# Third products, transposes and logits over all 128 rows of the array, in an mLSTM and mixture-of-experts kernel

## The chip, the cores and the metric

The kernel runs on one core of one Trainium2 chip. The metric is the device time of one execution in microseconds (us). A profile holds one execution, instruction by instruction: PE is TensorE's matmul, PEld its weight load (the stationary operand; it overlaps PE), DVE is VectorE, ACT ScalarE, POOL GpSimd, SP SyncE, which issues most DMAs. "L682" is a line of the kernel before.

## The reference

Two parts, in float32. First a recurrent attention (mLSTM) over batch 4, 8 heads, 768 steps, head size 40:

```python
    for t in range(S):
        m_new = np.maximum(f_gate[:, :, t] + m, i_gate[:, :, t])
        ...
        C = f_stab[:, :, None, None] * C + i_stab[:, :, None, None] * np.einsum('bhd,bhe->bhde', vt, kt)
        n = f_stab[:, :, None] * n + i_stab[:, :, None] * kt
        ...
        y[:, :, t] = o * h_tilde / denom
```

The eight heads side by side make 3072 tokens of 320 numbers. Each goes to one of 16 experts, in two choices of four (a group, then an expert in it), and through that expert's two layers:

```python
            h = np.maximum(xg[mask_e] @ w1[g, e], 0.0)
            ye = h @ w2[g, e]
            ...
            out[tok_idx] = combined[:, None] * ye
```

w1 is 320 x 1024 and w2 1024 x 320 for each expert.

## The kernel before, in words

A token's 320 columns are two blocks of 128 and one of 64. This third block is what the change is about.

**Attention.** The 768 steps are cut in 6 chunks of 128, for 4 batches: 24 units `u`, each 128 tokens. A unit makes scores (`sp`, L190), the carried state's part (`it`, L216), the new state (`st`, L236) and the values (`av`, L264) on TensorE; DVE and POOL mask and normalize, and `x` (L299) holds the finished tokens. `turn` (L302 on) lets ACT copy columns 256 to 319 once more to 320 to 383, stores the 384 columns in `x_d`, transposes `x` in three pieces (`tp`, L312; the third has 64 columns), and ACT copies them out to `xT` in two instructions (L318, L319). `logits` (L324 on) multiplies `xT` with `wc`, 20 columns, in three products (L333): xT is the stationary operand, and in the third it has 64 rows. `route` makes from four units' logits the choice, the rank in the expert (`lg`, L375 to L384) and the place in a table `itab`.

**Experts.** They are taken by falling number of tokens. `CAPS[r]` is the number of slots that the r-th gets: 384 (256 early and 128 late), 352, 320, 288, four of 256, four of 192, three of 160, and 128. The tokens of an expert are gathered in blocks of 128 slots (`load_x`, L593), the last block of some with fewer: 96 for expert 1, 64 for experts 2 and 8 to 11, 32 for 3 and 12 to 14. Slots that no token took hold the number of a row of zeros. `turn_tasks` transposes each gathered block (`tpm`, L648). Most experts then split x and w1 into two fp32r parts and use columns 256 to 319, doubled, against `wsk`. The experts in `FULL`, 13 to 15, don't: they multiply fp32 by fp32 in `expert` (L682), with three products per block of 128 hidden columns, of 128, 128 and 64 rows. Each fp32 product shows as two loads and two matmuls. Two blocks of hidden columns share a PSUM tile (`psh`, three buffers); ACT and DVE take the relu and its remainder from it (L668, L671), and a part of the next expert's w2 is split (`between`; L611, L613). Then come the next expert's transposes (`then`), and w2's products (`po`, L735 to L741).

**What sets the order.** Up to unit 21 the order is as written (`manual_schedule`); from there on a scheduler orders by its priorities. Each engine works through its own queue in order.

Of the kernel before, what the change touches and what calls it, by code (L numbers as in the profile page):

```python
# [18 lines left out]
P = 128  # L19
# [3 lines left out]
DM = H * D  # L23
NTOK = B * S
NE = 16
F = 1024
# [30 lines left out]
def lstm_moe(ctx: ExitStack, tc: tile.TileContext, gates, qkT, nat, og, wcat, w1, w2, cst, out):  # L57
    nc = tc.nc
    enter = ctx.enter_context
    mm = nc.tensor.matmul  # L60
# [3 lines left out]
    x_d = dram.tile([NTOK + 1, ROW], F32, name="x_d")  # L64
# [7 lines left out]
    ident = cs[:, C_ID:C_ID + P]  # L72
# [5 lines left out]
    wc = const.tile([P, 3, 20], F32, name="wc")  # L78
# [33 lines left out]
    rt = {"manual": True}  # L112
# [19 lines left out]
    st_ = {}  # L132
# [169 lines left out]
    def turn(u):  # L302
        c, b = divmod(u, B)
        x = st_[u]["x"]
        nc.scalar.copy(x[:, DM:DM + 64], x[:, 256:DM])
        rt["xs"] = ins = nc.sync.dma_start(x_d[b * S + c * P:b * S + (c + 1) * P, :], x)
        if c == NCH - 1:
            no_order("early", ins)
        tp = ps_1.tile([P, 3, P], F32, name="tp", tag="tp")
        for k in range(3):  # L310
            kk = min(P, DM - k * P)
            ins = nc.tensor.transpose(out=tp[0:kk, k, :], in_=x[:, k * P:k * P + kk], identity=ident)  # L312
        rt["tp", u] = ins
        if u > NU - 4:
            with tc.issue_after(ins.ins):
                busy(2)
        xT = wk.tile([P, 3, P], F32, name="xT")
        nc.scalar.copy(xT[:, 0:2, :], tp[:, 0:2, :])  # L318
        nc.scalar.copy(xT[0:64, 2, :], tp[0:64, 2, :])  # L319
        st_[u]["xT"] = xT  # L320


# [2 lines left out]
    def logits(u):  # L325
        c, b = divmod(u, B)
        if b == 0:
            rt["bank"] = ps_1.tile([P, B * 36 + NE], F32, name="lg")
        if u == NU - 1:
            rt["bank"] = ps_1.tile([P, B * 36 + NE], F32, name="lg2", tag="av")  # L330
        for k in range(3):
            kk = min(P, DM - k * P)
            rt["lg", u] = mm(rt["bank"][:, b * 20:(b + 1) * 20], st_[u]["xT"][0:kk, k, :], wc[0:kk, k, :],  # L333
                             start=(k == 0), stop=(k == 2))

        ends = {B - 1: 0} if c < NCH - 2 else {B - 2: 0, B - 1: B - 1}
        if b in ends:
            chores.insert(0 if c < NCH - 2 else len(chores), route(c, ends[b], b + 1, rt["bank"]))
# [90 lines left out]
    def no_order(key, ins):  # L429

        for o in unordered.setdefault(key, []):
            tc.declare_no_dep(ins.ins, o.ins, reason="distinct rows")
        unordered[key].append(ins)
# [116 lines left out]
    def gather(o, src, idx):  # L550
        return nc.gpsimd.indirect_dma_start(out=o, out_offset=None, in_=src,  # L551
                                            in_offset=bass.IndirectOffsetOnAxis(ap=idx, axis=0))
# [36 lines left out]
    def load_x(W, idx, early=False):  # L589
        xg = []  # L590
        for i, m in enumerate(blocks(W)):
            g = mxp.tile([P, ROW], F32, name="xg", bufs=9)
            ins = gather(g[0:m], x_d, idx(i, m)[:, 0:1])  # L593
            if early:

                no_order("early", ins)
            xg.append(g)
        return xg
# [37 lines left out]
    def turn_tasks(key, W, xg, banks=None):  # L636
        t = {}

        def one(i, m):
            if i == 0:  # L640
                pool = pools["xhl"][len(xhls) % len(pools["xhl"])]
                sh, dt = ([P, 3, W], F32) if key[0] in FULL else ([P, 3, 2, W], F32R)
                t["x"] = xhls[key] = pool.tile(sh, dt, name="xhl", bufs=1)
            xhl, g = t["x"], xg[i]
            pool, tag = (banks or ((ps_1, "tp"), (ps_1, "lg"), (ps_1, "av")))[i]
            tp = pool.tile([P, 3, P], F32, name="tpm", tag=tag)
            for k in range(3):
                nc.tensor.transpose(out=tp[:, k, 0:m], in_=g[0:m, k * P:(k + 1) * P], identity=ident[0:m, 0:m])  # L648
            if key[0] in FULL:
                nc.scalar.copy(xhl[:, :, i * P:i * P + m], tp[:, :, 0:m])  # L650
                return
            xh = xhl[:, :, 0, i * P:i * P + m]
            nc.scalar.copy(xh, tp[:, :, 0:m])
            nc.vector.tensor_tensor(xhl[:, :, 1, i * P:i * P + m], tp[:, :, 0:m], xh.bitcast(F32), op=ALU.subtract)

        return [lambda i=i, m=m: one(i, m) for i, m in enumerate(blocks(W))]

    def expert(key, W, ws, xg, idx, between=(), then=None, last=None):
        xhl = xhls[key]
# [15 lines left out]
        if key[0] in FULL:  # L675
            w1s = w1st[key[0]]
            for f in range(0, NF, 2):
                ps = pools["ps_h"].tile([P, 512], F32, name="psh")
                for g in range(2):
                    for k in range(3):  # L680
                        kk, s = min(P, DM - k * P), slice(k * F + (f + g) * P, k * F + (f + g + 1) * P)
                        ins = mm(ps[:, g * W:(g + 1) * W], w1s[0:kk, s], xhl[0:kk, k, :], start=(k == 0), stop=(k == 2))  # L682
                relu(f, 2, ps[:, 0:2 * W].rearrange("p (q w) -> p q w", q=2))
                do(between, 1)
        elif key in NARROW:
            xw, xh = [xhl[:, k].rearrange("p a w -> p (a w)") for k in range(3)], [xhl[:, k, 0, :] for k in range(2)]
            for f in range(0, NF, 2):
                hs = pools["hp"].tile([P, 2, W], F32, name="hs", bufs=2)
                for g in range(2):
                    ps = pools["ps_h"].tile([P, 512], F32, name="psh")  # L690
                    s0 = slice((f + g) * P, (f + g + 1) * P)
                    s1 = slice(F + (f + g) * P, F + (f + g + 1) * P)
                    mm(ps[:, 0:2 * W], w1h[:, s0], xw[0], start=True, stop=False)
                    mm(ps[:, 0:W], w1l[:, s0], xh[0], start=False, stop=False)
                    mm(ps[:, 0:W], w1l[:, s1], xh[1], start=False, stop=False)
                    mm(ps[:, 0:2 * W], w1h[:, s1], xw[1], start=False, stop=False)
                    ins = mm(ps[:, 0:2 * W], wsk[:, s0], xw[2], start=False, stop=True)
                    nc.scalar.copy(hs[:, g, :], ps[:, W:2 * W])
                    nc.vector.tensor_tensor(hs[:, g, :], hs[:, g, :], ps[:, 0:W], op=ALU.add)
                act = relu(f, 2, hs)  # L700
                if key[0] == 0:
                    do(between, 1)
        else:
            per = 2 if W <= 256 else 1
            for f in range(0, NF, per):
                ps = pools["ps_h"].tile([P, 512], F32, name="psh")
                for g in range(per):
                    s0 = slice((f + g) * P, (f + g + 1) * P)
                    s1 = slice(F + (f + g) * P, F + (f + g + 1) * P)
                    xh, xl = [xhl[:, k, 0, :] for k in range(3)], [xhl[:, k, 1, :] for k in range(3)]  # L710
                    todo = [(w1h, s0, xh[0]), (w1h, s0, xl[0]), (w1h, s1, xh[1]), (w1h, s1, xl[1]), (wsk, s0, xh[2]),
                            (wsk, s0, xl[2]), (w1l, s0, xh[0]), (w1l, s1, xh[1])]
                    for n, (w, s, x) in enumerate(todo):
                        ins = mm(ps[:, g * W:(g + 1) * W], w[:, s], x, start=(n == 0), stop=(n == len(todo) - 1))  # L714
                relu(f, per, ps[:, 0:per * W].rearrange("p (q w) -> p q w", q=per))
                if per == 2 or f % 2:
                    do(between, 1)
# [6 lines left out]
        for i, m in enumerate(blocks(W)):  # L724
# [3 lines left out]
            for f in range(NF):  # L728
                s = slice(f * DM, (f + 1) * DM)
# [4 lines left out]
                if m > 64:  # L734
                    mm(po[0:m], hh[:, f, t], w2h[:, s], start=st0, stop=False)  # L735
                    mm(po[0:m], hh[:, f, t], w2l[:, s], start=False, stop=False)  # L736
                    ins = mm(po[0:m], hh[:, f, tl], w2h[:, s], start=False, stop=sp0)  # L737
# [293 lines left out]
    with tc.For_i(0, nv, 1):  # L1031
# [25 lines left out]
        g = mxp.tile([P, ROW], F32, name="xg", bufs=9)  # L1057
        gather(g, x_d, ix[:, 0:1])
        w1s = wst.tile([P, 3 * F], F32, name="w1s")
# [3 lines left out]
        tp = ps_1.tile([P, 3, P], F32, name="tpm", tag="tp")  # L1063
        for k in range(3):
            nc.tensor.transpose(out=tp[:, k, :], in_=g[:, k * P:(k + 1) * P], identity=ident)
        xT = mxp.tile([P, 3, P], F32, name="xhl", bufs=1)
        nc.vector.tensor_copy(xT, tp)
        h = hp.tile([P, NF, P], F32, name="hh")
        for f in range(NF):
            ps = pools["ps_h"].tile([P, 512], F32, name="psh")  # L1070
            for k in range(3):
                kk = min(P, DM - k * P)
                mm(ps[:, 0:P], w1s[0:kk, k * F + f * P:k * F + (f + 1) * P], xT[0:kk, k, :], start=(k == 0),
                   stop=(k == 2))
# [12 lines left out]
def _lay(inputs):  # L1087
# [3 lines left out]
    q, k, v, o = (inputs[n] for n in ('q', 'k', 'v', 'o_gate'))  # L1091
# [12 lines left out]
    og = c(rows(o).reshape(NCH * B, P, DM).transpose(1, 0, 2))  # L1104
    wg, we = inputs['moe_w_group'], inputs['moe_w_expert']
    wcat = np.concatenate([wg, we.transpose(1, 0, 2).reshape(DM, NE)], axis=1)
    wcat = np.concatenate([wcat, np.zeros((3 * P - DM, 20), wcat.dtype)], axis=0)
    wcat = c(wcat.reshape(3, P, 20).transpose(1, 0, 2))
    w1 = inputs['moe_w1'].reshape(NE, DM, F)
    w1 = np.concatenate([w1, w1[:, 2 * P:]], axis=1)  # L1110
# [35 lines left out]
```

## Time and profile before

| | |
|---|---|
| median of 3 executions | 456.69 us (455.43 to 459.14) |
| the profiled execution | 457.81 us, span 456.2 us |
| mean granted TensorE clock | 0.977 |
| busy: PE, PEld | 426.2, 398.7 us |
| busy: DVE, ACT, POOL | 294.6, 253.8, 193.2 us |
| DMA | 94.75 MB, mean 208 GB/s |

How rows read: a group has line, engine, operation, output<-inputs, shapes and count, then busy us and mean ns of one, then the idle time just before and what ended it ("issue": nothing that the profile shows). For PE and PEld, "64*128" is rows times columns of the array that the stationary operand takes; the next "64x160" is the moving operand's partitions by elements. A row of a timeline has start and duration in us, and merges like instructions that follow each other under the first one's shape. A row of the waits has who waited for whom, us in total, how often, and the longest.

### The profile page before, as it was taken

The page shows a single profiled execution, that of the slowest core. Times are in us where ns is not written, and L with a number is a line of the kernel's source. Part 1 is how long each engine was busy: PE and PEld are TensorE (multiplying, and loading weights), DVE is VectorE, ACT ScalarE, POOL GpSimd, SP SyncE. Part 2 cuts the span into 40 slices and gives each one's busy share as a digit, 9 for nine tenths or more (in the row PEclk, how much of TensorE's full clock was granted, in tenths as well). Part 3 has the DMA queues.
Part 4 walks back from the last instruction along what each step waited for, and adds up shares of the span by engine and source line. Part 5 has one row for each costly group of instructions (what it writes and reads, how often), then busy time and mean ns, then how long its engine had stood idle before and what let it go on. Part 6 is the DMA issues. An engine that isn't in the chain of part 4 may idle for free.

```text
span 456.2 us, 9465 instructions
## 1 busy us (share of the span) xinstructions
PE 426.2 (93%) x3420; PEld 398.7 (87%) x3420; DVE 294.6 (65%) x737; ACT 253.8 (56%) x587; POOL 193.2 (42%) x216
## 2 busy tenths in 40 slices
PE   7589999997987999699999999999999999999995
PEld 4489999897987997498999999999999999988784
DVE  6746877658768897495747584676656876772510
ACT  5557666483674842446637464657565765672411
POOL 7544566565564563337713415303330663130110
PEclk9989999998998999599999999999999999999999
DMA  4999797997799922347995536658665776344000
GB/s 153 289 290 284 248 242 227 282 239 247 206 324 298 321 70 60 144 156 215 366 379 185 202 120 236 214 190 293 211 222 187 281 250 218 133 147 141 14 15 10
DMA packets 29909, 94.75 MB, mean 208 GB/s; under 512 B 9169, under 2 KB 13226, under 8 KB 26276
## 3 DMA queue, kind: packets, MB, share of 16 engines
q1 hardware_dynamic: 24660, 78.28, 53.2%
q0 software_dynamic: 4928, 15.49, 10.0%
q8 instruction: 28, 0.46, 0.5%
q10 hardware_dynamic: 272, 0.36, 0.3%
q14 instruction: 21, 0.17, 0.1%
HBM read 84.14 MB, written 10.82 MB: 208 GB/s over the span
## 4 chain that ended last, share of the span: by engine, by line
PE 56%; issue 20%; POOL 11%; DVE 6%; DMA 3%; ACT 2%; POOLq 1%; ACTq 0%; DVEq 0%
PE psh L714 20%; PE po L735 6%; PE po L736 6%; PE po L737 6%; PE sp L190 4%; PE tpm L648 2%; POOL itab L458 2%; POOL sr L293 2%; DMA qk<-in_qkT_dram 2%; PE it L216 2%; PE po L741 2%; POOL ab L152 2%; DMA xg<-x_d,ix 1%; POOL kw L203 1%; PE po L740 1%
## 5 line engine op out<-in xcount | busy, mean ns | idle before, releaser
L551 POOL DMA_INDIRECT xg<-x_d,ix x34 | 41.6, 1223 | 109.0 <-DMA ix<-itab 65.5
L555 POOL DMA_INDIRECT out_dram<-y,ix x34 | 40.8, 1200 | 60.7 <-ACT y L747 42.8
L735 PE MATMUL po<-w2h,hh 128*128 128x320 f32 (+1 forms) x208 | 65.8, 317 | 0.0
L737 PE MATMUL po<-w2h,hh 128*128 128x320 f32 (+1 forms) x208 | 64.2, 309 | 0.0
L736 PE MATMUL po<-w2l,hh 128*128 128x320 f32 (+1 forms) x208 | 64.2, 309 | 0.0
L613 DVE TENSOR_TENSOR w2l<-w2s,w2h 128x640 fp32r<-128x640 f32 x64 | 50.2, 817 | 20.5 <-ACT w2h L611 20.4
L180 ACT ACTIVATE ab<-ab,bcol 128x128 f32<-128x128 f32 x184 | 56.3, 388 | 12.8 <-POOL ab L152 12.3
L714 PE MATMUL psh<-xhl,w1h 128*128 128x256 f32 (+4 forms) x352 | 59.5, 290 | 0.2 <-DVE sm L390 0.2
L671 DVE SCALAR_TENSOR_TENSOR hh<-psh,hh 128x256 fp32r<-128x256 f32 (+2 forms) x104 | 39.5, 411 | 24.3 <-ACT hh L668 23.9
L668 ACT ACTIVATE hh<-psh 128x512 fp32r<-128x512 f32 (+5 forms) x68 | 33.4, 491 | 38.7 <-PE psh L714 21.3
L190 PE MATMUL sp<-qk 128*128 128x128 f32 x384 | 50.8, 287 | 4.4 <-DMA qk<-in_qkT_dram 4.4
L264 PE MATMUL av<-nt,pt 128*128 128x128 f32 x384 | 51.4, 287 | 0.8 <-DVE pt L196 0.7
L190 PEld LDWEIGHTS sp<-qk 128*128 128x128 f32 x384 | 47.2, 199 | 5.2 <-issue 2.6
L714 PEld LDWEIGHTS psh<-xhl,w1h 128*128 128x128 f32 x352 | 50.5, 192 | 1.2 <-ACT ex L357 1.0
L264 PEld LDWEIGHTS av<-nt,pt 128*128 128x128 f32 x384 | 46.3, 196 | 2.2 <-DVE pt L196 1.2
L152 POOL TENSOR_SCALAR_AFFINE_SELECT ab<-ab 128x1024 f32<-128x1024 f32 (+1 forms) x25 | 27.2, 1089 | 48.0 <-DMA ab<-a_d 43.6
L611 ACT CAST w2h<-w2s 128x640 fp32r<-128x640 f32 x64 | 43.2, 723 | 0.0
L735 PEld LDWEIGHTS po<-w2h,hh 128*128 128x128 f32 (+1 forms) x208 | 38.8, 187 | 0.8 <-ACT hh L668 0.2
L196 DVE TENSOR_TENSOR pt<-sp,ab 128x512 f32<-128x512 f32 x48 | 32.8, 684 | 9.8 <-PE sp L190 8.0
L613 DVE TENSOR_TENSOR w1l<-w1s,w1h 128x1024 fp32r<-128x1024 f32 x26 | 31.7, 1219 | 11.1 <-ACT w1h L611 8.8
L736 PEld LDWEIGHTS po<-w2l,hh 128*128 128x128 f32 (+1 forms) x208 | 38.9, 187 | 0.0
L737 PEld LDWEIGHTS po<-w2h,hh 128*128 128x128 f32 (+1 forms) x208 | 38.8, 187 | 0.0
(177 smaller groups left out, 873.4 us busy)
## 6 DMA issues: line engine op xcount, KB each, us to landing
w1s<-in_w_dram SPq DMA_DIRECT2D x12, 1536.0 KB
w2s<-in_w_dram SPq DMA_DIRECT2D x12, 1280.0 KB
ab<-a_d SPq DMA_DIRECT2D x23, 512.0 KB
nt<-in_nat_dram SPq DMA_DIRECT2D x24, 324.0 KB
qk<-in_qkT_dram SPq DMA_DIRECT2D x48, 160.0 KB
x_d<-x SPq DMA_DIRECT2D x24, 192.0 KB
sig<-in_og_dram SPq DMA_DIRECT2D x6, 640.0 KB
w1s<-in_w_dram SPq DMA_DIRECT2D x4, 768.0 KB
```

The lines of the kernel that those rows point to most:

```text
L180: rt["exp"] = nc.scalar.activation(ab[:, j, :], ab[:, j, :], AF.Exp, bias=bcol[:, c, b * H + j:b * H + j + 1])
L190: mm(sp[:, jj, :], qk[:, j % 2, j // 2, :], qk[:, 2, j // 2, :], start=True, stop=True)
L264: mm(av[:, o:o + P], t["pm"][j // 4][:, j % 4, :], nt[:, o:o + P], start=True, stop=True)
L551: return nc.gpsimd.indirect_dma_start(out=o, out_offset=None, in_=src, in_offset=bass.IndirectOffsetOnAxis(ap=idx, axis=0))
L555: return nc.gpsimd.indirect_dma_start(out=out, out_offset=bass.IndirectOffsetOnAxis(ap=idx, axis=0), in_=y, in_offset=None, bounds_check=N ...
L611: nc.scalar.copy(a, src[:, s])
L613: lows.append(lambda: nc.vector.tensor_tensor(o[rows], src[rows, s], a[rows].bitcast(F32), op=ALU.subtract))
L671: nc.vector.scalar_tensor_tensor(hh[:, f:f + per, dst], src[:, :, t], 0.0, hr.bitcast(F32)[:, :, t], op0=ALU.max, op1=ALU.subtract)
L714: ins = mm(ps[:, g * W:(g + 1) * W], w[:, s], x, start=(n == 0), stop=(n == len(todo) - 1))
L735: mm(po[0:m], hh[:, f, t], w2h[:, s], start=st0, stop=False)
L736: mm(po[0:m], hh[:, f, t], w2l[:, s], start=False, stop=False)
L737: ins = mm(po[0:m], hh[:, f, tl], w2h[:, s], start=False, stop=sp0)
```

## The change

`turn` transposes three times 128 columns; the third piece begins at column 192, so that columns 192 to 255 come twice. One copy brings all to `xT`. `wcat` gets its 64 rows of zeros ahead of the last 64 rows instead of behind them, so the doubled columns meet zeros, and all three logit products have 128 rows. Short blocks of slots are gathered with 128 rows, and transposed as 128 x 128; only the first `m` columns of the result are copied out, as before. In FULL experts the third piece of a gathered token holds columns 256 to 319 twice, and w1's third part has those rows twice already; DVE sets rows 64 to 127 of the third piece of `xhl` to zero, and the third product has 128 rows.

```diff
-        for k in range(3):
-            kk = min(P, DM - k * P)
-            ins = nc.tensor.transpose(out=tp[0:kk, k, :], in_=x[:, k * P:k * P + kk], identity=ident)
+        for k, s in enumerate((0, P, DM - P)):
+            ins = nc.tensor.transpose(out=tp[:, k, :], in_=x[:, s:s + P], identity=ident)
...
-        nc.scalar.copy(xT[:, 0:2, :], tp[:, 0:2, :])
-        nc.scalar.copy(xT[0:64, 2, :], tp[0:64, 2, :])
+        nc.scalar.copy(xT, tp)
...
-            kk = min(P, DM - k * P)
-            rt["lg", u] = mm(rt["bank"][:, b * 20:(b + 1) * 20], st_[u]["xT"][0:kk, k, :], wc[0:kk, k, :],
-                             start=(k == 0), stop=(k == 2))
+            rt["lg", u] = mm(rt["bank"][:, b * 20:(b + 1) * 20], st_[u]["xT"][:, k, :], wc[:, k, :], start=(k == 0),
+                             stop=(k == 2))
...
-            ins = gather(g[0:m], x_d, idx(i, m)[:, 0:1])
+
+            ins = gather(g, x_d, idx(i, P)[:, 0:1])
...
-                nc.tensor.transpose(out=tp[:, k, 0:m], in_=g[0:m, k * P:(k + 1) * P], identity=ident[0:m, 0:m])
+                nc.tensor.transpose(out=tp[:, k, :], in_=g[:, k * P:(k + 1) * P], identity=ident)
             if key[0] in FULL:
                 nc.scalar.copy(xhl[:, :, i * P:i * P + m], tp[:, :, 0:m])
+
+                nc.vector.memset(xhl[DM - 2 * P:, 2, i * P:i * P + m], 0.0)
                 return
...
-                        kk, s = min(P, DM - k * P), slice(k * F + (f + g) * P, k * F + (f + g + 1) * P)
-                        ins = mm(ps[:, g * W:(g + 1) * W], w1s[0:kk, s], xhl[0:kk, k, :], start=(k == 0), stop=(k == 2))
+                        s = slice(k * F + (f + g) * P, k * F + (f + g + 1) * P)
+                        ins = mm(ps[:, g * W:(g + 1) * W], w1s[:, s], xhl[:, k, :], start=(k == 0), stop=(k == 2))
...
-    wcat = np.concatenate([wcat, np.zeros((3 * P - DM, 20), wcat.dtype)], axis=0)
+    wcat = np.concatenate([wcat[0:2 * P], np.zeros((3 * P - DM, 20), wcat.dtype), wcat[2 * P:]], axis=0)
```

The order of the instructions stays the same nearly everywhere. On PE it differs where the scheduler works at the end of the attention. The last unit's logits (`lg_2554` before, `lg_2530` after) and the rank products of the units before it (`lg<-oh`) stand there, ahead of the first experts' transposes. Before:

```order
L333 MATMUL lg_2554<-wc,xT 128x20 x2
L119 LDWEIGHTS ones_b
L119 MATMUL busy<-ones_b 128x512
L375 LDWEIGHTS lt_b
L375 MATMUL lg<-oh,lt_b 128x48
...
L379 MATMUL lg<-ohsum_77,ones_b 128x48
L333 MATMUL lg_2554<-wc,xT 128x20
L648 MATMUL tpm<-cs,xg 128x128 x6
```

And now:

```order
L119 LDWEIGHTS ones_b
L119 MATMUL busy<-ones_b 128x512
L373 LDWEIGHTS lt_b
L373 MATMUL lg<-oh,lt_b 128x48
...
L377 MATMUL lg<-ohsum_77,ones_b 128x48
L331 MATMUL lg_2530<-wc,xT 128x20 x3
L647 MATMUL tpm<-cs,xg 128x128 x6
```

The first two logit products moved behind the rank products, to the third.

On DVE the clears of `xhl` are new. The first two stand in expert 12, while its last `hs` (sums of two parts of `psh`) and `hh` (remainders of the relu) are made; `xhl` is that of expert 13. Before:

```order
L671 SCALAR_TENSOR_TENSOR hh<-hs,hh 128x2x32
L699 TENSOR_TENSOR hs<-hs,psh 128x160 x2
L671 SCALAR_TENSOR_TENSOR hh<-hs,hh 128x2x128
L671 SCALAR_TENSOR_TENSOR hh<-hs,hh 128x2x32
L613 TENSOR_TENSOR w2l<-w2s,w2h 128x640 x4
```

And now:

```order
L672 SCALAR_TENSOR_TENSOR hh<-hs,hh 128x2x32
L700 TENSOR_TENSOR hs<-hs,psh 128x160 x2
L651 MEMSET xhl 64x128
L672 SCALAR_TENSOR_TENSOR hh<-hs,hh 128x2x128
L672 SCALAR_TENSOR_TENSOR hh<-hs,hh 128x2x32
L651 MEMSET xhl 64x32
L612 TENSOR_TENSOR w2l<-w2s,w2h 128x640 x4
```

Each clear waits for ACT's copy of the same block; the two remainders of expert 12's last hidden columns stand behind the first.

## The prediction

> **What bounds the kernel now.** I read the page first, then the busy times by stretch, the instructions by shape, the weight loads in order of time, the chain and the waits. The page's busy row and its chain:
>
> ```profile
> PE 426.2 (93%) x3420; PEld 398.7 (87%) x3420; DVE 294.6 (65%) x737; ACT 253.8 (56%) x587; POOL 193.2 (42%) x216
> PE 56%; issue 20%; POOL 11%; DVE 6%; DMA 3%; ACT 2%; POOLq 1%; ACTq 0%; DVEq 0%
> ```
>
> TensorE leads in both. The stretches (busy us of PE, in the second row also PEld, DVE, ACT, POOL, then granted clock, DMA share, GB/s) separate two regimes:
>
> ```profile
> 30.00:182.00 152.00, 140.60 (x1390) 0.98 0.79 237
> 200.00:456.00 256.00, 249.78 (x1766) 235.94 (x1765) 152.31 (x293) 136.09 (x257) 84.58 (x71) 1.00 0.56 195
> ```
>
> In the attention (30 to 182) PE lacks 11.4 of 152 us and DMA is busy 0.79 of the time; in the experts (200 to the end) PE is occupied nearly throughout and DVE, ACT, POOL and DMA have room. A busy PE is not one at its peak, so I looked at its loads by shape (the first number of "64*128" is rows of the array) and at the stretch of the FULL experts, which multiply x and w1 unsplit:
>
> ```profile
> L682 PEld LDWEIGHTS psh<-xhl,w1s 128*128 128x128 f32 x96 | 13.4, 189 | 3.3 <-issue 2.4
> L682 PEld LDWEIGHTS psh<-xhl,w1s 64*128 64x128 f32 x48 | 7.1, 184 | 3.7 <-issue 2.7
> L714 PEld LDWEIGHTS psh<-xhl,wsk 128*128 128x128 f32 x176 | 27.9, 191 | 0.0
> ```
> ```profile
> 406.16 0.61 PEld L682 LDWEIGHTS psh<-xhl,w1s 128*128 128x128 f32 x4
> 406.94 0.29 PEld L682 LDWEIGHTS psh<-xhl,w1s 64*128 64x128 f32 x2 [0.17 <-issue]
> 407.41 0.57 PEld L682 LDWEIGHTS psh<-xhl,w1s 128*128 128x128 f32 x4 [0.17 <-issue]
> 408.15 0.29 PEld L682 LDWEIGHTS psh<-xhl,w1s 64*128 64x128 f32 x2 [0.17 <-issue]
> 408.62 0.57 PEld L682 LDWEIGHTS psh<-xhl,w1s 128*128 128x128 f32 x4 [0.17 <-issue]
> ```
>
> A 64-row load itself lasts no longer than a 128-row one (184 against 189 ns). But at every passage from 128 rows to 64, and at every passage back, the loader stands 0.17 us with no releaser, and what it would have hidden shows. The third product of the other experts has 128 rows (wsk, L714) and no idle time at all over 176 loads. So the pause goes with the change of row count, not with the third product as such. Each fp32 product is two loads and two matmuls, hence x4 and x2.
>
> **Part by part.** *FULL experts, third products at 128 rows (L682).* The matmuls, first from two short windows and then whole:
>
> ```profile
> 406.31 0.57 PE L682 MATMUL psh<-xhl,w1s 128*128 128x160 f32 x3
> 406.31 0.70 PE L682 MATMUL psh<-xhl,w1s 128*128 128x160 f32 x4
> 406.31 9.62 PE L682 MATMUL psh<-xhl,w1s 128*128 128x160 f32 x48
> 422.60 2.71 PE L682 MATMUL psh<-xhl,w1s 128*128 128x160 f32 x13
> 438.40 8.42 PE L682 MATMUL psh<-xhl,w1s 128*128 128x128 f32 x48
> ```
>
> Within one row count a further 160-wide matmul adds 0.70 - 0.57 = 0.13 us. Over all 48 of expert 13 the mean step is (9.62 - 0.57) / 45 = 0.20. With no change of row count it saves 45 x 0.07 = about 3.1 us. Expert 14 has the same shapes and count; its first 13 take 2.71 us (0.2 a step), so 3.1 again. Expert 15 is 128 wide. A 128-wide fp32 matmul at full pace is in the rows below (16 in 1.79 us, 0.112 each). Its 48 should take 5.4 instead of 8.4: 3.0 us. Together 9.2; I take 9.0, because the last step out of each phase may keep a pause.
>
> Does anything else become the bound there? One pair of column blocks (12 matmuls) falls from 2.4 to 1.6 us, and this is what ACT and DVE do for one in expert 14, relu and weight split:
>
> ```profile
> 425.16 0.44 ACT L668 ACTIVATE hh<-psh 128x320 fp32r<-128x320 f32 x1
> 425.50 0.72 ACT L611 CAST w2h<-w2s 128x640 fp32r<-128x640 f32 x1
> 425.63 0.56 DVE L671 SCALAR_TENSOR_TENSOR hh<-psh,hh 128x256 fp32r<-128x256 f32 x2
> 426.10 0.81 DVE L613 TENSOR_TENSOR w2l<-w2s,w2h 128x640 fp32r<-128x640 f32 x1
> ```
>
> That is 1.16 us on ACT and 1.37 on DVE, under 1.6: late next is DVE, by 0.2 us to spare. Expert 15 has no split. So the 9 us stay on PE's line to the end. If the two engines took turns instead of overlapping, a pair would need 0.44 + 0.72 + 0.81 + 0.56 = 2.5 us, and experts 13 and 14 would gain nothing (6 us of the 9).
>
> *The five clears of xhl (DVE).* The nearest row is a memset six times as wide:
>
> ```profile
> L881 DVE MEMSET R__118<- 32x768 f32 x1 | 0.7, 698 | 0.1
> ```
>
> At most 0.7 us each. For experts 14 and 15 they fall between one expert's first products and the next one's: expert 13's end at 415.9 by the rows above, expert 14's begin at 422.6. The third product now waits for them, 6 us after. For expert 13 they stand in expert 12's DVE queue; behind them wait two hh subtractions, and PE's second products for those. I take nothing, and 0.7 at worst.
>
> *Gathered blocks transposed at 128 rows (L648).* Six transposes up to the first second-layer product, for two full blocks and for a full one and one of 64 rows:
>
> ```profile
> 300.56 0.81 PE L648 MATMUL tpm<-cs,xg 128*128 128x128 f32 x6
> 301.13 0.40 PE L735 MATMUL po<-w2h,hh 128*128 128x320 f32 x1
> 331.12 0.82 PE L648 MATMUL tpm<-cs,xg 128*128 128x128 f32 x6
> 331.87 0.41 PE L735 MATMUL po<-w2h,hh 128*128 128x320 f32 x1
> ```
>
> From the first transpose to L735: 0.57 and 0.75 us, so 0.18 saved although more columns stream. Five blocks have 64 rows and four have 32 (priced alike): 9 x 0.18 = 1.6 us, on a full PE. The one block of 96 rows streams a quarter more in three matmuls of 0.11 us: under 0.1 us lost.
>
> *Gathers of 128 rows (L551).* They bring 736 more rows of 1.5 KB, 1.1 MB. At the 195 GB/s of the second stretch that is 6 us of traffic, spread over 256 us in which DMA is busy 0.56. POOL issues as many gathers as before.
>
> ```profile
> DMA to landing us min/median/max: 3.1/6.6/15.0
> ```
>
> Only the second expert's third block (96 rows before) is fetched shortly before use. A third more of 3.1 to 6.6 us would land 1 to 2 us late, once. I take nothing, since all other blocks are fetched experts ahead, and keep 2 us for the range.
>
> *Logits at 128 rows (L333).* From the chain:
>
> ```profile
> 58.45 1.98 PE sp L190 x16
> ...
> 61.29 0.72 PE lg L333 x6
> ...
> 64.75 1.79 PE sp L190 x16
> ```
>
> The scores behind logits (58.45) take 0.19 us longer than the same 16 behind transposes (64.75). The six logit matmuls take 0.72 where six at 0.112 make 0.67. So about 0.24 a unit, 24 units: 5.8 us if PE's line were all that counted. It isn't, because PE also waits:
>
> ```profile
> PE sp L190 <- DMA qk<-in_qkT_dram: 4.4, 2, 2.5
> PE lg L375 <- DVE oh L370: 3.7, 3, 2.4
> PE tp L312 <- DVE x L299: 2.6, 4, 1.5
> PEld st L236 <- POOL kw L203: 2.6, 2, 1.9
> ```
>
> Eleven waits (second number). If the work behind such a wait doesn't depend on PE's earlier pace, the saving of that unit is lost in it; 13 units are left, 13 x 0.24 = 3.1 us. I take 3.0, with 0 (DMA or the other engines set the pace all along) and 5.8 as ends.
>
> *Third transposes of a unit, and one copy for two.*
>
> ```profile
> L318 ACT COPY xT<-tp 128x256 f32<-128x256 f32 x24 | 8.8, 367 | 14.2 <-PE tp L312 14.2
> L319 ACT COPY xT<-tp 64x128 f32<-64x128 f32 x24 | 6.2, 258 | 0.0
> L650 ACT COPY xhl<-tpm 128x384 f32<-128x384 f32 x3 | 1.4, 481 | 0.1
> ```
>
> These transposes already had 128 rows and only 64 columns, so there was no passage to remove. The copy falls from 0.625 to 0.48 us on ACT, but the first logit can start 0.11 later than with the 0.367 copy. Logits mostly come a unit later, so I take zero; the ends are 24 x 0.14 = 3.4 us gained and 24 x 0.11 = 2.6 lost. The last unit's third logit, which stood alone behind the rank products, now has the other two beside it there; the rank products no longer stand behind them.
>
> **The sum.** 9.0 + 1.6 + 3.0 = 13.6 us. The profiled execution took 457.8 us (span 456.2 and 1.6 around it), so 444.2 in its own measure. It lies 1.1 above the median of 456.7, so 443 as a median.
>
> **A rule against the change.** The loads of 64 and 128 rows last 184 and 189 ns, as above. The Trainium skill, "TensorE: Matmul & The Clock Gate", section "LDWEIGHTS (loading the stationary operand)", says that loading time goes with the columns and that a 32x128 load takes as long as a 128x128 one. On the duration the trace agrees; by that rule alone the FULL term would be 0 instead of 9.0, and the forecast about 457. On the passages the trace sides with another page, "TensorEngine Tiling (Array Packing)", section "Key Properties": changing the tiling mode drains TensorE.
>
> **Rivals.** *The pauses stay.* The 0.17 us could belong to something else that stays, the jump to w1's third part or the end of a sum, and nothing comes off PE: about 457, no change. Against it stand the 176 loads of wsk without idle time, and the transposes, another tile in another place, which lose 0.18 too. Chance 0.05; the rule on columns above would come to the same.
>
> *DVE or ACT becomes the bound in the FULL experts.* Then 6 of the 9 us go and 449 is left. For it: DVE has only 0.2 us a pair to spare. Against: psh has three buffers, and the two engines overlap in the rows. Chance 0.05.
>
> *Slower, by the clock.* This row is a stretch in the attention at half clock:
>
> ```profile
> 107.50:110.90 3.40, 3.40 (x18) 3.36 (x17) 3.25 (x17) 1.98 (x9) 0.00 (x0) 0.50 0.96 352
> ```
>
> Such a window costs 1.7 us. Less work on PE in the attention means longer waits there, and if these bring more such windows, PE pays. It needs 13.6 / 1.7 = 8 new ones to lose the gain and 11 to be slower by 1%: about 462. Against: the change adds 0.24 us to a wait, and the clock over 30 to 182 is 0.98 although the longest waits are 2.5 us. One more or one less is likely, eleven are not. Chance 0.02.
>
> **The numbers.** The main case has 0.88: 443, and by its own ends 438 (all of the attention's 5.8, some of ACT's, one half-clock window less) to 449 (nothing from the attention, one window more, the gather 2 us late). The second rival ends at 449 as well. 1%, 4.6 us, is about what a measurement of this kernel can tell from no change. Faster by over 1%: 0.88 + 0.05 less a little for errors of size, 0.92. Within: 0.05. Slower: 0.03.
>
> **What would show it.** After the change no L682, logit or transpose load should have 64 or 32 rows, and the 0.17 us idle times should be gone. 48 matmuls of a FULL expert should take 6.5 us (160 wide) and 5.4 (128 wide); if they still take 9.6, the first step is wrong. DVE or ACT as the releaser of the first products there would mean the second rival. In the attention, a unit without waits should be 0.24 us shorter; if PE's waits grow by as much as its work shrinks, the 3.0 is wrong. More rows at clock 0.50 would be the third rival.

## The result, and the profile after

The changed kernel took 444.29 us in the median of four executions (438.66 to 448.51), the kernel before 456.06 beside it (454.28 to 459.14): ratio 0.9648, 95% interval 0.9537 to 0.9759. Run twice more, it stood at 0.9719 (0.9677 to 0.9760) and 0.9726 (0.9667 to 0.9785), which is 12 to 13 us off. The forecast was 443.0, or 13.6 us off. Medians here are over all executions; the ratios leave disturbed ones out, so the two need not agree to the last digit.

The profiled execution took 441.97 us. Its busy row and its chain:

```profile
PE 413.2 (94%) x3420; PEld 396.7 (90%) x3420; DVE 295.8 (67%) x742; ACT 251.8 (57%) x563; POOL 192.5 (44%) x216
PE 60%; issue 12%; DMA 10%; DVE 7%; POOL 6%; ACT 2%; POOLq 1%; SPq 1%; DVEq 0%
```

PE has the same 3420 instructions and is busy 13.0 us less. "issue", the time for which the profile has no releaser, falls from 20% of the chain to 12%. The stretches of the attention and of the experts:

```profile
30.00:178.00 148.00, 138.48 (x1402) 0.98 0.80 238
200.00:440.00 240.00, 233.64 (x1730) 229.06 (x1728) 147.70 (x284) 135.03 (x256) 80.42 (x68) 1.00 0.58 205
```

The regimes are as they were: in the experts PE is occupied nearly throughout at full clock, in the attention it still lacks some 10 us. The loads by shape, for the FULL experts and the logits:

```profile
L683 PEld LDWEIGHTS psh<-xhl,w1s 128*128 128x128 f32 x144 | 18.6, 191 | 0.0
L331 PEld LDWEIGHTS lg<-wc,xT 128*128 128x128 f32 x144 | 18.4, 196 | 2.7 <-DVE pr L401 1.7 <-ACT xT L317 1.0
```

No load of 64 rows is left in either. The FULL loads lost all of their 3.3 + 3.7 us of idle time; what the logits' loads still have is waits for DVE and ACT. The three FULL experts' first products, 48 matmuls each:

```profile
399.93 6.68 PE L683 MATMUL psh<-xhl,w1s 128*128 128x160 f32 x48
...
412.98 6.68 PE L683 MATMUL psh<-xhl,w1s 128*128 128x160 f32 x48
...
425.69 5.52 PE L683 MATMUL psh<-xhl,w1s 128*128 128x128 f32 x48
```

They took 9.62, 9.62 and 8.42. And a full and a short gathered block, up to the first second-layer product:

```profile
325.88 0.82 PE L647 MATMUL tpm<-cs,xg 128*128 128x128 f32 x6
326.46 0.40 PE L736 MATMUL po<-w2h,hh 128*128 128x320 f32 x1
```

That is 0.58 us from start to start, where a short block had taken 0.75.

To see what the experts give together, take two marks that both traces have: the start of the first expert's second group of transposes, and the start of the last expert's first products. Before and after:

```profile
205.55 0.49 PE L648 MATMUL tpm<-cs,xg 128*128 128x128 f32 x3
...
438.40 8.42 PE L682 MATMUL psh<-xhl,w1s 128*128 128x128 f32 x48
```
```profile
200.70 0.55 PE L647 MATMUL tpm<-cs,xg 128*128 128x128 f32 x3 [0.33 <-DMA xg<-x_d,li]
```

From mark to mark it was 232.85 us and is now 425.69 - 200.70 = 224.99, 7.86 less; with the last expert's own 2.90, 10.8 us. That is close to the forecast's 9.0 + 1.6 = 10.6. The first mark itself came 4.85 us earlier, but what comes before it can't be read from one trace: in kernels whose attention is unchanged the same mark lay at 205.55 (the kernel before), 204.00, 202.16 and 201.16 us (three kernels of the experiments: half the passages, the FULL part alone, the short blocks alone), with stretches at half clock in differing places. For that part timed comparisons are needed.

### The profile page after: what moved, and what is told of

It is laid out like the page before. It is cut to its first block, busy times and chain, and to the rows that moved or that the text cites. A ratio compares the mean times of both kernels' runs of the same rounds, so it can differ in the third digit from the quotient of the medians.

```text
span 440.2 us, 9445 instructions
## 1 busy us (share of the span) xinstructions
PE 413.2 (94%) x3420; PEld 396.7 (90%) x3420; DVE 295.8 (67%) x742; ACT 251.8 (57%) x563; POOL 192.5 (44%) x216
## 2 busy tenths in 40 slices
DMA packets 30131, 95.86 MB, mean 218 GB/s; under 512 B 9169, under 2 KB 13146, under 8 KB 26500
## 3 DMA queue, kind: packets, MB, share of 16 engines
q0 software_dynamic: 5152, 16.62, 10.6%
## 4 chain that ended last, share of the span: by engine, by line
PE 60%; issue 12%; DMA 10%; DVE 7%; POOL 6%; ACT 2%; POOLq 1%; SPq 1%; DVEq 0%
PE psh L715 18%; PE po L736 5%; PE po L738 5%; PE po L737 5%; PE sp L190 5%; PE av L264 5%; DMA qk<-in_qkT_dram 3%; DMA ab<-a_d 3%; PE tpm L647 3%; PE it L216 2%; PE po L742 2%; DMA xg<-x_d,ix 1%; PE lg L331 1%; PE po L741 1%; DMA xg<-x_d,li 1%
## 5 line engine op out<-in xcount | busy, mean ns | idle before, releaser
L549 POOL DMA_INDIRECT xg<-x_d,ix x34 | 40.1, 1181 | 108.3 <-DMA ix<-itab 51.1
L553 POOL DMA_INDIRECT out_dram<-y,ix x34 | 42.2, 1242 | 47.0 <-ACT y L748 29.8
L264 PE MATMUL av<-nt,pt 128*128 128x128 f32 x384 | 52.8, 292 | 2.3 <-DVE pt L196 2.3
L190 PEld LDWEIGHTS sp<-qk 128*128 128x128 f32 x384 | 48.2, 203 | 4.0 <-DMA qk<-in_qkT_dram 2.9
L264 PEld LDWEIGHTS av<-nt,pt 128*128 128x128 f32 x384 | 47.5, 200 | 4.0 <-DVE pt L196 3.0
```

The costliest lines, as they stand in the source:

```text
L190: mm(sp[:, jj, :], qk[:, j % 2, j // 2, :], qk[:, 2, j // 2, :], start=True, stop=True)
L264: mm(av[:, o:o + P], t["pm"][j // 4][:, j % 4, :], nt[:, o:o + P], start=True, stop=True)
L553: return nc.gpsimd.indirect_dma_start(out=out, out_offset=bass.IndirectOffsetOnAxis(ap=idx, axis=0), in_=y, in_offset=None, bounds_check=N ...
```

## The experiments

The theory is that of the forecast: each passage of the array from 128 rows to 64 or 32 and each passage back costs PE time (by the forecast about 0.2 us in the FULL experts, 0.12 among the logits), and the change removes the passages. The rival of most weight is that something else of the change brings the gain (the order, the single copy), or that one of the three parts carries all of it.

**One part at a time.** The first kernel is the one before with the FULL part alone:

```diff
+                nc.vector.memset(xhl[DM - 2 * P:, 2, i * P:i * P + m], 0.0)
...
-                        ins = mm(..., w1s[0:kk, s], xhl[0:kk, k, :], ...)
+                        ins = mm(..., w1s[:, s], xhl[:, k, :], ...)
```

> The FULL part alone (third products of experts 13 to 15 over 128 rows, with the clears); logits, transposes and gathers are those of before. If each passage between 64 and 128 rows costs a pause and nothing else takes its place: 48 matmuls in about 6.5 us (160 wide, two experts) and 5.4 us (128 wide), 9 us less than before in all. If DVE or ACT becomes the bound there: 3 us less. If the pauses belong to the third product as such: no change.

Measured: 444.88 us (442.09 to 449.73), ratio 0.9765 (0.9724 to 0.9806), so 10.7 us off (8.8 to 12.6). The first products of two of its FULL experts:

```profile
402.87 6.68 PE L683 MATMUL psh<-xhl,w1s 128*128 128x160 f32 x48
...
428.78 5.52 PE L683 MATMUL psh<-xhl,w1s 128*128 128x128 f32 x48
```

These are the changed kernel's durations; the three phases lose 2.94 + 2.94 + 2.90 = 8.8 us. This part alone carries most of the gain.

The second kernel has the attention's part alone: the third transpose of 128 columns, one copy, the moved zeros of `wcat`, and logits of 128 rows.

> The attention part alone (three transposes of 128 columns, one copy, logits over 128 rows). The logits' pauses go, 0.24 us in each of 24 units. If half of the units keep what they save: 3 us less. If PE's line is the only bound: 5.8 us less. If DMA or the other engines set the pace, or the saving is given back in waits and half-clock windows: within 1 us of before.

Measured: 454.15 us (449.71 to 459.96), ratio 0.9959 (0.9918 to 1.0000), 1.9 us off (0 to 3.7). No gain at all lies at the edge of this interval.

The third has the gathers and transposes of short blocks with 128 rows alone:

```diff
-            ins = gather(g[0:m], x_d, idx(i, m)[:, 0:1])
+            ins = gather(g, x_d, idx(i, P)[:, 0:1])
...
-                nc.tensor.transpose(out=tp[:, k, 0:m], in_=g[0:m, ...], identity=ident[0:m, 0:m])
+                nc.tensor.transpose(out=tp[:, k, :], in_=g[:, ...], identity=ident)
```

> Gathers and transposes of short blocks with 128 rows alone. If a passage of rows costs 0.17 us there as elsewhere, nine blocks save 0.18 each: 1.6 us less in the experts. If the wider gathers land late: the second expert's blocks are waited for, and the time is within 1 us of before or above it.

Measured: 451.96 us (448.90 to 457.18), ratio 0.9916 (0.9872 to 0.9960), 3.8 us off (1.8 to 5.8). In the trace, from expert 1's transposes to the first FULL products, of the kernel before and of this one:

```profile
212.40 1.07 PE L648 MATMUL tpm<-cs,xg 128*128 128x128 f32 x9
```
```profile
208.07 1.15 PE L648 MATMUL tpm<-cs,xg 128*128 128x128 f32 x9
...
400.50 9.62 PE L682 MATMUL psh<-xhl,w1s 128*128 128x160 f32 x48
```

Against the earlier row of 406.31, that is 193.91 us before and 192.43 now: 1.48 us. Eight of the nine short blocks lie in this stretch, and 8 x 0.18 = 1.4 was forecast for them. So the trace bears out the price, but not the whole of the 3.8: some 2 us of it are unexplained, and the forecast's 1.6 lies just below the interval. In these two traces everything else lies ahead of this stretch, where single executions differ by as much (the marks above); whether the wider gathers do something there is open. The three parts add to 16.4 us, the whole measured 12.4 to 16.0; the intervals, about 2 us each way for every part, cover that.

**Half the passages.** The next kernel keeps 64 rows and the work, and only turns the order of products in every second block, so that third products of two blocks stand side by side:

```diff
-                    for k in range(3):
+                    for n, k in enumerate((2, 0, 1) if g else (0, 1, 2)):
...
-                        ins = mm(..., start=(k == 0), stop=(k == 2))
+                        ins = mm(..., start=(n == 0), stop=(n == 2))
```

> The kernel before, with the products of each second block of hidden columns in FULL experts in the order third, first, second: the 64-row products of two blocks stand side by side, still of 64 rows, and there are half as many passages between row counts. If the passage costs the time: half of the FULL experts' gain, 4.5 us less than before. If a 64-row product is slow in itself, or the third product as such: no change.

Measured: 451.03 us (444.96 to 453.41), ratio 0.9885 (0.9835 to 0.9934), 5.2 us off (3.0 to 7.5). The loads and the 48 matmuls of expert 13:

```profile
405.48 0.57 PEld L682 LDWEIGHTS psh<-xhl,w1s 64*128 64x128 f32 x4 [0.17 <-issue]
406.21 1.11 PEld L682 LDWEIGHTS psh<-xhl,w1s 128*128 128x128 f32 x8 [0.17 <-issue]
```
```profile
404.85 8.25 PE L682 MATMUL psh<-xhl,w1s 128*128 128x160 f32 x48
```

There are as many loads of 64 rows as before, but the pause stands once for four of them. The phase lost 1.37 us with half of its 16 passages gone and 2.94 with all of them gone. So in the FULL experts it is the passage that costs, about 0.17 to 0.18 us each, and not the 64-row product: "the pauses stay" and any account by row count alone fall here. So does the rule of the Trainium skill, "TensorE: Matmul & The Clock Gate", section "LDWEIGHTS (loading the stationary operand)", taken as a forecast of no gain: a load's duration goes with the columns, as the rows of the FULL experts say (184 to 191 ns at 64, 96 and 128 rows), but the throughput does not.

**96 rows.** The changed kernel with third products of 96 rows in FULL experts, and clears of 32 rows:

```diff
-                        s = slice(k * F + (f + g) * P, k * F + (f + g + 1) * P)
-                        ins = mm(..., w1s[:, s], xhl[:, k, :], ...)
+                        kk, s = 96 if k == 2 else P, slice(k * F + (f + g) * P, k * F + (f + g + 1) * P)
+                        ins = mm(..., w1s[0:kk, s], xhl[0:kk, k, :], ...)
```

> The changed kernel with 96 rows in the third products of FULL experts instead of 128 (w1's third part and x cut at row 96; rows 64 to 95 cleared). If what counts is whether a product fits in half of the rows: 96 rows pass like 128, 48 matmuls step over 6.4 us (160 wide) and 5.2 (128 wide), as in the changed kernel. If any other row count is a passage: 9.3 and 8.2 us, as before the change.

Measured, in a single execution: 440.69 us. Its loads by shape, and the matmuls:

```profile
L683 PEld LDWEIGHTS psh<-xhl,w1s 128*128 128x128 f32 x96 | 13.8, 189 | 0.0
L683 PEld LDWEIGHTS psh<-xhl,w1s 96*128 96x128 f32 x48 | 7.7, 191 | 0.0
```
```profile
398.61 6.71 PE L683 MATMUL psh<-xhl,w1s 128*128 128x160 f32 x48
```

Between 96 and 128 rows there is no pause (6.71 against 6.68 us). The kernel before shows the same at its gathered blocks: no idle time ahead of the loads of expert 1's 96 rows, but some ahead of those of 32 rows:

```profile
L648 PEld LDWEIGHTS tpm<-cs,xg 32*128 32x128 f32 x12 | 1.0, 136 | 0.7 <-issue 0.5 <-DMA xg<-x_d,ix 0.2
L648 PEld LDWEIGHTS tpm<-cs,xg 96*128 96x128 f32 x3 | 0.3, 141 | 0.0
```

The cost belongs to passages to 64 and 32 rows, not to any change of the row count.

**The attention: more passages.** To price a passage there, this kernel adds to the one before a 64-row product by zeros between the first and the second logit product. That makes two more passages and two more matmuls a unit:

```diff
-        for k in range(3):
+        for n, (k, kk, wt) in enumerate(((0, P, wc[:, 0, :]), (2, 64, zc), (1, P, wc[:, 1, :]), (2, 64, wc[:, 2, :]))):
...
-            rt["lg", u] = mm(..., st_[u]["xT"][0:kk, k, :], wc[0:kk, k, :], start=(k == 0), stop=(k == 2))
+            rt["lg", u] = mm(..., st_[u]["xT"][0:kk, k, :], wt[0:kk], start=(n == 0), stop=(n == 3))
```

> The kernel before with one more 64-row product by zeros in each unit's logits, between the first and the second product: two more passages and two more matmuls, about 0.5 us of PE a unit, 12 us over 24 units. The output is the same. If PE's line sets the attention's pace: 12 us slower than before. If half of the units lose their saving in waits, as the prediction had it: 6 us slower. If DMA or the other engines set it: within 1.5 us of before.

Measured: 466.10 us (461.74 to 472.62), ratio 1.0174 (1.0124 to 1.0223), 7.9 us more (5.6 to 10.2). One unit of it, then the same unit of the kernel before, then of the changed kernel, from the start of one unit's 16 scores to the next one's:

```profile
65.36 2.05 PE L191 MATMUL sp<-qk 128*128 128x128 f32 x16
...
68.10 0.34 PE L333 MATMUL lg<-wc,xT 128*128 128x20 f32 x2
68.37 0.40 PE L333 MATMUL lg<-zc,xT 64*128 64x20 f32 x2
68.69 0.72 PE L333 MATMUL lg<-wc,xT 128*128 128x20 f32 x4
69.35 0.51 PE L237 MATMUL st<-nt,kw 128*40 128x41 f32 x16
...
72.00 0.72 PE L191 MATMUL sp<-qk 128*128 128x128 f32 x5
```
```profile
57.51 0.95 PE L333 MATMUL lg<-wc,xT 128*128 128x20 f32 x6 [0.39 <-DVE pr L403]
58.38 2.05 PE L190 MATMUL sp<-qk 128*128 128x128 f32 x16
...
61.12 0.88 PE L333 MATMUL lg<-wc,xT 128*128 128x20 f32 x6
61.94 0.51 PE L236 MATMUL st<-nt,kw 128*40 128x41 f32 x16
...
64.59 0.61 PE L190 MATMUL sp<-qk 128*128 128x128 f32 x4
```
```profile
57.06 0.84 PE L331 MATMUL lg<-wc,xT 128*128 128x20 f32 x6 [0.39 <-DVE pr L401]
57.75 2.03 PE L190 MATMUL sp<-qk 128*128 128x128 f32 x16
...
60.47 0.78 PE L331 MATMUL lg<-wc,xT 128*128 128x20 f32 x6
61.19 0.51 PE L236 MATMUL st<-nt,kw 128*40 128x41 f32 x16
61.62 2.05 PE L264 MATMUL av<-nt,pt 128*128 128x128 f32 x16
...
63.84 0.83 PE L190 MATMUL sp<-qk 128*128 128x128 f32 x6
```

The unit takes 6.21 us before, 6.64 in this kernel and 6.09 after the change. The added 0.43 in each of 24 units would be 10.3 us; 7.9 arrived, so some three quarters of what is added to PE in the attention reaches the time (0.54 to 0.99 by the interval). The forecast had let 13 units of 24 count, 0.54. Of the 0.43 us the two matmuls take 2 x 0.112 = 0.22 at the pace of the logits, which leaves 0.1 us for each of the two passages: here a passage costs little more than half of what it costs in the FULL experts. Why is open.

The same rows show what the change saves in a unit. Where scores follow the logits, from the first logit to the first score: 0.87 us before, 0.69 after, 0.18 saved. Where the state products `st` follow: 0.82 before, 0.72 after, only 0.10 saved. Six logits at 0.112 make 0.67, so ahead of the scores next to nothing of a pause is left, and ahead of `st` about 0.05 us.

**Is it the column halves of `st`?** The products of odd heads go to partitions 64 to 103 of their PSUM tile, those of even heads to 0 to 39. If changing the half makes the pause that remains, it should go when all go to partition 0:

```diff
-                mm(st[r0:r0 + D, pr, :], t["kw"][:, j, :], nt[:, j * D1:(j + 1) * D1], start=True, stop=True)
+                mm(st[0:D, j, :], t["kw"][:, j, :], nt[:, j * D1:(j + 1) * D1], start=True, stop=True)
```

> The changed kernel with the state products (L236, 40 columns each) of the odd heads written to PSUM partitions 0 to 39 like the even heads', instead of 64 to 103. If the pause of about 0.08 us that PE still makes between the logits and these products comes of their two halves of the array's columns: it goes, six logits up to the first state product take 0.63 us instead of 0.71, and the sixteen state products, which no longer overlap in pairs, take longer than 0.43 us. If it comes of 40 columns being fewer than 128: it stays at 0.71.

Measured, in a single execution: 445.12 us.

```profile
58.81 0.78 PE L330 MATMUL lg<-wc,xT 128*128 128x20 f32 x6
59.52 0.81 PE L235 MATMUL st<-nt,kw 128*40 128x41 f32 x16
60.26 2.05 PE L263 MATMUL av<-nt,pt 128*128 128x128 f32 x16
```

The 0.71 us up to the first `st` stay (0.72 in the changed kernel), so it is not the halves. But the 16 products now take 0.74 us up to the first of the values (`av`), instead of 0.43.

**The changed kernel again, and fillers.** In the first trace of the changed kernel PE waits for 4.9 us for the first expert's gather, up to 183 us, and the mean clock from 176 to 186 us is 0.67. The next kernel has 20 filler matmuls instead of 4 behind the last logits, and issues the first expert's transposes behind them; the one after it has six more fillers behind those transposes.

```diff
-    busy(4)
+    with tc.issue_after(rt["lg", NU - 1].ins):
+        busy(20)
...
-    with tc.issue_after(rt["lg", NU - 1].ins), tc.high_priority():
+    with tc.issue_after(rt["busy"].ins), tc.high_priority():
```

> The changed kernel once more, beside the others of this call. If the parts add up: the FULL part's 2.35%, the blocks' 1.58 us in the experts and the attention's 0 to 2 us make 11 to 14 us less than before. If they share one resource: less than the FULL part and the blocks alone, under 10 us.

> The changed kernel with 20 filler matmuls (bf16, 512 wide) instead of 4 while PE waits for the first expert's gathered tokens, and these transposes behind them. If the half clock there (7 to 10 us long, from 178 us on) comes of PE's wait of 2 to 5 us: it stays away, and 2 to 4 us less than the changed kernel. If the clock falls for another reason, or the fillers delay the transposes: no change, or 1 to 2 us slower than the changed kernel.

> As the kernel with 20 fillers, and 6 more behind the transposes, where PE waited 1.2 us and the clock then halved for 3.4 us. If the half clock comes of PE's waits: none from 176 to 200 us, and 1 to 2 us less than with 20 fillers, 3 to 5 less than the changed kernel beside it. If not: as with 20 fillers or slower.

> The changed kernel beside the one with 26 fillers: about 12.8 us less than before, as in its run above (0.972), if that figure is not chance.

Measured side by side: changed kernel 442.86 us, ratio 0.9719 (0.9677 to 0.9760), with 20 fillers 440.86, ratio 0.9646 (0.9597 to 0.9695). And side by side once more: changed kernel 443.63, ratio 0.9726 (0.9667 to 0.9785), with 26 fillers 440.46, ratio 0.9665 (0.9596 to 0.9735). Busy times by stretch between the attention and the experts: in the first fence the changed kernel and then, in two rows, the one with 20 fillers beside it; in the second the changed kernel of the other comparison; in the third the one with 26 fillers. The column behind the five engines is the clock:

```profile
176.00:186.00 10.00, 4.69 (x24) 3.00 (x22) 3.37 (x24) 2.45 (x5) 3.87 (x4) 0.59 0.54 184
```
```profile
176.00:186.00 10.00, 7.40 (x47) 3.96 (x47) 8.85 (x48) 6.37 (x12) 6.70 (x6) 1.00 0.55 192
186.00:190.00 4.00, 3.53 (x17) 3.53 (x18) 3.63 (x9) 1.08 (x2) 0.76 (x1) 0.59 0.01 1
```
```profile
186.00:190.00 4.00, 4.00 (x19) 2.92 (x18) 3.00 (x17) 3.94 (x5) 0.00 (x0) 0.50 0.03 4
```
```profile
176.00:186.00 10.00, 9.34 (x55) 5.22 (x53) 8.69 (x39) 6.41 (x10) 5.61 (x5) 0.87 0.42 156
186.00:190.00 4.00, 4.00 (x36) 4.00 (x35) 4.00 (x11) 1.19 (x2) 0.79 (x1) 1.00 0.09 1
```

With 20 fillers the clock was 1.00 where it had been 0.59, and fell to 0.59 in the next 4 us. With 26 it was 1.00 in these 4 us, where it had been 0.50, but 0.87 in the 10 us before, although PE was busy for 9.34 of them. So the expectation of no low clock from 176 to 200 us failed, and what lowers the clock there is not settled. Both versions were 2 to 3 us ahead of the changed kernel beside them in the median, but the intervals overlap in both comparisons. A version that beats the changed kernel is likely and not shown, and the six further fillers brought nothing that could be told apart.

## Why the prediction was right, and where it was not

**FULL experts, 9.0 us: right.** The phases lost 2.94, 2.94 and 2.90 us where 3.1, 3.1 and 3.0 were worked out (6.68 and 5.52 us for 48 matmuls by the rows, where 6.5 and 5.4 were to be seen). Counted up to the start of PE's next instruction they are 6.52 and 5.28 us, and the losses 3.03, 3.03 and 3.07. Alone the part measured 10.7 (8.8 to 12.6). Both halves of the argument hold: the idle time of 0.17 us goes with the passage (half the passages, half the gain), and nothing takes its place.

**DVE or ACT as the bound there (449 us): refuted.** All 144 loads of L683 follow without idle time, so PE did not wait for `psh`. ACT's relus of expert 14 keep PE's pace at 0.44 us each for a pair that takes PE 1.6:

```profile
416.49 0.44 ACT L669 ACTIVATE hh<-psh 128x320 fp32r<-128x320 f32 x1
```

**Clears of xhl, 0: right, and cheaper than the bound.** Where 0.7 us was the end, the five took

```profile
L651 DVE MEMSET xhl<- x5: 85/165/165, 394.5 to 420.8; 64x128 f32 x3, 64x32 f32 x2
```

85 to 165 ns, ending microseconds before the products that read them.

**Short blocks, 1.6 us: right in the trace.** 1.48 us for eight of the nine (1.4 by the forecast), with one block at 0.58 us where 0.75 stood. The timed 3.8 us (1.8 to 5.8) is more than that price explains.

**Gathers, 0 with 2 in the range: 0 as far as a trace shows.** The DMAs moved 95.86 MB, 1.1 more. In the list of waits after the change PE waits for gathers of the first expert alone: once for 4.9 us, up to 183 us, where the kernel before waits as well, and once for 0.3 us for its late block, which had 128 rows before, too:

```profile
PE tpm L647 <- DMA xg<-x_d,ix: 4.9, 1, 4.9
...
PE tpm L647 <- DMA xg<-x_d,li: 0.3, 1, 0.3
```

The second expert's third block is not among them.

**Logits, 3.0 us: near the mark by luck, two errors that offset each other.** The step that was off is "about 0.24 a unit, 24 units". It adds 0.19 us of scores behind logits and 0.05 us of logits ahead of `st`, which are two kinds of unit, and applies the sum to all. Nor was the 0.19 all passage: in the rows above the scores behind logits take 2.05 us before and still 2.03 after, and what is saved lies ahead of their start. Over the attention of the two traces, logits stand ahead of `st` in 13 units, where 0.10 is saved, and ahead of scores or values in some nine, where about 0.20 is: 3.1 us of PE's work instead of 5.8. The other step, that only 13 units in 24 count because 11 waits swallow theirs, was probably too low: 0.54 is the lower end of what the run with more passages allows, 0.77 its middle. 3.1 x 0.77 = 2.4 us, and the part measured 1.9 (0 to 3.7), the wider transposes and the single copy included. The share was measured with work added; that it holds for work taken away was not shown. The copy took 0.473 us, where 0.48 was worked out. That copy and transposes cost or bring nothing fits the 1.9, but no run separated them from the logits.

**Slower by the clock (462 us): it did not come.** The kernel became 12 to 16 us faster, and the stretch of the attention has the same mean clock as before, 0.98. Eight more windows at half clock, 1.7 us lost in each, would have brought it down to about 0.89 (13.6 of 148 us).

**The sum.** 13.6 us was forecast; 16.0 (11.0 to 21.1 from the interval), 12.8 and 12.4 were measured in three comparisons. The terms as the traces and the share have them are 8.8 + 1.5 + 2.4 = 12.7. One figure of the forecast was loose: with the FULL term alone at 0 it would have been 443 + 9.0 = 452; the 457 given there needs all three terms at 0. The measured 444.29 fits neither.

## What to carry to other kernels

Look in the weight loads for idle time without a releaser and see which shapes stand on both sides of it: a short contraction among full ones can be cheaper padded to the full array with zeros, or, if that can't be done, sorted so that short products stand together. Price such a pause at each place where it stands, since here it was 0.17 to 0.18 us a passage in the FULL experts and 0.1 among the logits. Where an engine leads but also waits, measure the share that arrives by adding a known amount of its work to every unit: here that gave 0.77 (0.54 to 0.99), where counting the waits gave 0.54.

## What the runs showed of the hardware

Third products of 96 rows passed among those of 128 without a pause (6.71 against 6.68 us for 48), while 64 rows paused at each passage, and blocks of 32 rows paused, too. The Trainium skill, "TensorEngine Tiling (Array Packing)", section "Key Properties", has it that a change of the tiling mode drains TensorE; the trace agrees for 64 and 32 rows, at 0.17 to 0.18 us a passage in the FULL experts and some 0.1 us among the logits, and shows no pause between 96 and 128.

Behind logits of full height, state products with a stationary operand of 40 columns still began later than the pace of the logits (0.72 us for six at 0.112), also when all of them wrote to partition 0. What makes that pause is open.

Sixteen products of 40 columns took 0.43 us when they alternated between PSUM partitions 0 and 64, and 0.74 when all went to partition 0.

A lower clock also came where PE waited for little. In the kernel with 20 fillers these two stand ahead of the 4 us at 0.59 (in brackets the wait):

```profile
184.76 0.55 PE L647 MATMUL tpm<-cs,xg 128*128 128x128 f32 x3 [0.94 <-DMA xg<-x_d,ix]
186.47 1.05 PE L715 MATMUL psh<-xhl,w1h 128*128 128x256 f32 x4 [1.16 <-DVE xhl L655]
```

That they are its cause was not tested by itself. With 26 fillers the clock was 0.87 over 10 us in which PE stood idle for 0.66 us.
